# A transformer kernel on one core: thirty-two recorded orders instead of one, a rearranged head, column tiles from segment one, a last product cut 512 + 128

## The chip, the cores and the metric

One core of one Trainium2 chip runs the kernel. Its engines run on their own and wait for each other by semaphores: TensorE (PE for matmuls, PEld for weight loads), VectorE (DVE), ScalarE (ACT), GpSimd (POOL) and SyncE (SP, which here issues nearly all DMAs). The metric is device microseconds of one execution; before the change the median of three runs is 577.09 us (575.79 to 577.29).

## The reference

Two layers, each an attention with a compressive memory and a feed-forward part, on 2048 tokens of width 640, all in bf16. The tokens are cut in four segments of 512.

```python
def _A_ref(x, wq, wk, wv, wo, beta):          # 32 heads of 20, N = 4 segments of L = 512
    for s in range(N):
        logits = einsum('bhqd,bhkd->bhqk', qs, ks) * scale + mask      # causal, inside the segment
        a_dot = einsum('bhqk,bhkd->bhqd', softmax(logits), vs)
        pq = phi(qs)                                                   # t > 0 ? t + 1 : exp(t)
        a_mem = (pq @ M) / (pq . z + 1e-06)                            # memory of earlier segments
        outs.append(g * a_mem + (1.0 - g) * a_dot)                     # g = sigmoid(beta), per head
        pk = phi(ks); M = M + pk^T vs; z = z + sum(pk)
    return concat(outs) @ wo
def _B_ref(x, w1, w2):
    return relu(x @ w1) @ w2                                           # 640 -> 1728 -> 640

x = x + _A_ref(_layernorm(x), wq, wk, wv, wo, beta)
x = x + _B_ref(_layernorm(x), w1, w2)
# and both once more, with the same weights
```

## The kernel before

**Recorder.** The program is not written in the order in which it runs. Some thirty Python generators ("streams") each describe one kind of work for all eight (layer, segment) pairs: scores, exponentials, causal masks, values, output projection, normalization, projections, feed-forward and so on. A stream yields an `Op` (engine, planned duration, tokens that it waits for), a `Need` (an event that another stream sets) or an `Acq` (a buffer slot). `Sched.run` keeps a planned clock for each engine and, step by step, takes the op that could start earliest; among equal starts the lower number given in `S.add` goes first. It appends the op to that engine's list with its semaphore waits (`Prog`). The order on each engine, and on SP's DMA queue, is therefore fixed by planned times, and each engine then runs its list strictly in order.

Some rules bend that choice. An op of PE that is not a score is held back (`late`) until what it waits for has been done for a guard time, `TRUST_NS` (0.4 us for ACT, DVE and POOL, 1 us for a DMA). A matmul block in another tiling mode than the last costs `SWITCH_NS` more; blocks in column tiles are held up to 4 us to join a score block. Where the plan leaves PE idle for 0.3 us or more, `keep_busy` puts small matmuls on the identity there (L594).

**Work.** PSUM has eight banks: two pairs (X, Y) for scores and four (`MISC`) for all else; the memory read uses one of those alone. A segment's attention goes in four steps (`m`) of two half-groups of four heads (`z`), each step in five rounds of scores (L1067, four heads side by side in row tiles), exponentials on ACT (L1119) and causal selects on POOL (L1131). Then come the values. In segments 0 and 1 of the first layer (`BY_TOKEN`) this is `values_by_token`: 40 matmuls of 21 columns per half-group (L1161), which leave numbers and denominators by token, and DVE divides straight from PSUM (L1173, L1174, L1177). In all others `apply` computes the transposed result with 16 matmuls in four column tiles (L1210), evacuates it to `av` (L1218 DVE or L1219 ACT), a DMA transpose on SP turns it to `avt` (L638), and `divide` works from there (L1246, L1247, L1254). `combine` adds the memory part (L1272). After that come turn_o, the output projection, the second normalization and the feed-forward product.

The memory read is L960, L968, L970 and L971, its update L1011 to L1032. Queries and keys go through a scratch tensor in HBM (`spill`, L856; `fill`, L903) into padded tiles `pad`, four slots; only the first heads go straight there (L883). `group` (L607 first matmul, L610 the rest) is the helper for all other products, `add_half` (L1281) adds a product to the residual, and L1379 stores a finished token tile.

**Head.** `first_ln_a` normalizes token tiles 0 and 1: statistics of both (L618, L620), one `lnU` (L628), one power on POOL (L632), two normalizations (L672). `first_ln_b` does tiles 2 and 3 with their statistics on ACT (L722, L729, then L630). PE transposes all four (L695), ACT or DVE evacuates them (L702, L701), and the projections begin. `consts` makes the constants: identity (L540), the mask `maskg` (memset L547, ten selects L552 and L555), the ones in the value tiles (memsets L562 and L564), the gates (L569 to L581). `warm_pe` (L590) runs 60 matmuls to begin with.

Of the kernel before, what the change touches and what calls it, by code (L numbers as in the profile page):

```python
# [11 lines left out]
H = 32  # L12
# [146 lines left out]
SWITCH_NS = 97.0  # L159
JOIN_NS = 4000.0  # L160
# [8 lines left out]
class Sched:  # L169


    def __init__(self, prog):
        self.P = prog
        self.free = {e: 800.0 for e in ENGS}
        self.t = {}
        self.events = {}
        self.streams = []
        self.dma_free = 0.0
        self.pe_mode = "full"
        self.spare = []  # L180
        self.idle_fn = None

    def keep_busy(self, op, start):
# [10 lines left out]
        if n > 1:  # L194
            self.P.waits("pe", s.tks)
            for _ in range(n):
                self.P.op("pe", lambda e, ap=s.ap: self.idle_fn(e, ap), False)
# [45 lines left out]
    def _alts(self, op):  # L243
# [7 lines left out]
        for k, (e, hold, fns, tail) in enumerate(op.alts):  # L251
            m = PE_MARGIN if e == "pe" else 0.0
            if e == "pe" and op.mode != self.pe_mode:
                hold = hold + SWITCH_NS
            start = max([self.at(t) + SEM_NS + m for t in waits], default=0.0)
            start = max(self.free[e], start)
            res.append((start + hold, start, k, e))
        return res

    def run(self):  # L260
        while True:
# [21 lines left out]
            for prio, n, st, alts, op, late in heads:  # L283
# [4 lines left out]
                if prio > 0 and alts and alts[0][3] == "pe":  # L288
                    sure = max([self.at(t) + TRUST_NS[self.P.lane(t)] for t in op.waits], default=0.0)
# [28 lines left out]
            if e == "pe":  # L318
                self.keep_busy(op, start)
            self.P.waits(e, waits)  # L320
# [10 lines left out]
            else:  # L331
# [6 lines left out]
                out = marks[0] if len(marks) == 1 else (marks or None)  # L338
            st[2], st[3] = None, ((slot, out) if slot is not None else out,)

# [31 lines left out]

def bass_interleave_layers__memory_aug_infini_attn__dense_activation_relu__prompt_kernel(
    nc, A_x, A_wq, A_wk, A_wv, A_wo, A_beta, B_x, B_w1, B_w2, out,
):
    with contextlib.ExitStack() as es:
        sb = lambda name, shape, dtype=dt.bfloat16: es.enter_context(nc.sbuf_tensor(name, shape, dtype))
        sem_ = lambda name: es.enter_context(nc.semaphore(name))
        P = Prog({e: sem_("clk_" + e) for e in ["act", "dve", "pool", "pe"]})
        S = Sched(P)  # L380


        NPAD, NXT, NXN, NPT = 4, 2, 2, 2
        wq_r = sb("wq_r", [128, FC, D])
        wk_r = sb("wk_r", [128, FC, D])
        wv_r = sb("wv_r", [128, FC, D])
        wo_r = sb("wo_r", [128, FC, D])
        w1_r = sb("w1_r", [128, FC, DFF])
        w2_r = sb("w2_r", [128, NDC, D])
        w2_u = sb("w2_u", [128, D])  # L390
        ident = sb("ident", [128, 128])
        warm = sb("warm", [128, 1], dt.float32)
        asum = sb("asum", [128, 4], dt.float32)
        beta_bc = sb("beta_bc", [128, H])
        gt = sb("gt", [128, 3, H], dt.float32)
        omg = sb("omg", [128, G, NJ, 4, 1], dt.float32)
        maskg = sb("maskg", [128, MW])
        stats6 = sb("stats6", [128, TT, 2, 6], dt.float32)
        mv = sb("mv", [128, TT, 2], dt.float32)
        rstd = sb("rstd", [128, TT], dt.float32)  # L400
        lnU = sb("lnU", [128, TT], dt.float32)
        mhalf = sb("mhalf", [128, 4], dt.float32)
        x_sb = sb("x_sb", [128, TT, D])
        xnT = sb("xnT", [128, NXT, NJ * FC, 128])
        xn_tok = sb("xn_tok", [128, NXN, 2 * D])
        stg = sb("stg", [128, FC, 2, L])
        phs = sb("phs", [128, FC * L])
        pad = sb("pad", [128, NPAD, 2, 2, L])
        rtmp = sb("rtmp", [128, 3, L])
        phk = sb("phk", [128, FC, NJ, 128])  # L410
        v_aug = sb("v_aug", [128, 2, NJ, H, DH + 1])
        M_sb = sb("M_sb", [128, MW], dt.float32)
        BD = sb("BD", [128, MW])
        PT = sb("PT", [128, NPT, 4, PTH])
        o_sb = sb("o_sb", [128, NJ, D])
        om_sb = sb("om_sb", [128, NJ, D])
        rden = sb("rden", [128, 2, 2 * NJ, 4, 1], dt.float32)
        av = sb("av", [128, 2, L])
        avt = sb("avt", [128, 2 * NJ, 128])
        rmem = sb("rmem", [128, 4, 16, 1], dt.float32)  # L420
        oT = sb("oT", [128, NJ * FC, 128])
        hT = sb("hT", [128, NFULL, L])
        hL = sb("hL", [128, 2 * 128])
        ps = es.enter_context(nc.psum_tensor("ps", [128, 8, 512], dt.float32))

        X = Slot(ps[:, 0:2, :], "SX")
        Y = Slot(ps[:, 2:4, :], "SY")
        MISC = [Slot(ps[:, 4 + k, :], "misc%d" % k) for k in range(4)]
        XNT_A = [Slot(xnT[:, k], "xnT_a") for k in range(1)]
        XNT_B = [Slot(xnT[:, k], "xnT_b") for k in range(1, NXT)]  # L430
        XN = [Slot(xn_tok[:, k], "xn") for k in range(NXN)]
        xn_sem = {id(s): sem_("xn%d" % k) for k, s in enumerate(XN)}
        early_w = w2_r[:].rearrange("p c d -> p (c d)")
        VLEN = NJ * H * (DH + 1)
        STGS = [stg, early_w[:, VLEN:VLEN + 2 * FC * L].rearrange("p (c n t) -> p c n t", c=FC, n=2)]
        STG = [[[Slot(ap[:, c, n], "stg") for c in range(FC)] for n in range(2)] for ap in STGS]
        PAD = [Slot(pad[:, k], "pad") for k in range(NPAD)]
        pad_sem = {id(s): sem_("pad%d" % k) for k, s in enumerate(PAD)}
        scr = nc.dram_tensor("scr", [2, D, 2 * L], dt.bfloat16, kind="Internal").ap()
        scr_sem = [[sem_("scr%d_%d" % (n, c)) for c in range(FC)] for n in range(2)]  # L440
        RT = [Slot(rtmp[:, k], "rt") for k in range(3)]
        PARTS = ((0, 1, 2), (3, 4))
        PHK = [Slot(phk[:, cs[0]:cs[-1] + 1], "phk") for cs in PARTS]
        PHS = [Slot(phs[:, cs[0] * L:(cs[-1] + 1) * L], "phs") for cs in PARTS]
        VAUG = [v_aug[:, k] for k in range(2)]
        VAUG += [early_w[:, 0:VLEN].rearrange("p (j h e) -> p j h e", j=NJ, e=DH + 1)]
        VA = [Slot(ap, "va") for ap in VAUG]
        BDS = Slot(BD, "bd")
        PTS = [Slot(PT[:, k], "pt") for k in range(NPT)]
        OSB = Slot(o_sb[:], "osb")  # L450
        OMS = [Slot(om_sb[:, :, 320 * k:320 * k + 320], "om") for k in range(2)]
        RDEN = [Slot(rden[:, k], "rden") for k in range(2)]
        AV = Slot(av[:], "av")
        AVT = Slot(avt[:], "avt")
        avt_sem = sem_("avt")
        RMEM = [[Slot(rmem[:, 2 * n + k], "rmem") for k in range(2)] for n in range(2)]
        OT = [Slot(oT[:, 2 * FC * k:2 * FC * k + 2 * FC], "oT") for k in range(2)]
        ot_sem = {id(s): sem_("ot%d" % k) for k, s in enumerate(OT)}
        phk_sem = [sem_("phk%d" % p) for p in range(2)]
        HT = Slot(hT, "hT")  # L460
        XNT_E = [Slot(hT[:, FC * k:FC * k + FC, :].rearrange("p c (i n) -> p (c i) n", n=128), "xnT_e")
                 for k in range(2)]


        def ld(e, name, nbytes, fn, waits=()):
            tk = yield dma(e, sem_("d_" + name), nbytes, fn, waits, lat=2200.0)
            S.set(name, tks=[tk])

        def wload(e, name, w, src, waits=()):
            yield from ld(e, name, 819200, lambda eng: eng.dma_start(  # L470
                w[:], src.rearrange("(c p) d -> p c d", p=128)), waits)

        xs = A_x[0].rearrange("(t p) d -> p t d", p=128)

        def loads():
            def x_pair(name, t):
                yield from ld("sp", name, 327680, lambda e: e.dma_start(x_sb[:, t:t + 2, :], xs[:, t:t + 2, :]))

            def cols(name, w, src, c0, c1):
                yield from ld("sp", name, 1280 * (c1 - c0), lambda e: e.dma_start(  # L480
                    w[:, :, c0:c1], src.rearrange("(c p) d -> p c d", p=128)[:, :, c0:c1]))

            yield from x_pair("x00", 0)
            yield from x_pair("x01", 2)
            yield from cols("wk0", wk_r, A_wk, 0, 256)
            yield from cols("wq0", wq_r, A_wq, 0, 256)
            yield from cols("wk1", wk_r, A_wk, 256, D)
            yield from cols("wq1", wq_r, A_wq, 256, D)
            yield from wload("sp", "wv", wv_r, A_wv)
            yield from x_pair("x10", 4)  # L490
            yield from x_pair("x11", 6)

# [244 lines left out]
        def proj_ln(a, s):  # L737
            if (a, s) == (0, 0):
                return
# [720 lines left out]
```

## Time and profile before

| | |
|---|---|
| median of three runs | 577.09 us (575.79 to 577.29) |
| the profiled execution's own time | 575.81 us |
| its span, first to last instruction | 573.8 us |
| mean granted TensorE clock | 0.997 |
| PE busy | 564.1 us, 98% of the span |
| PEld, DVE, ACT, POOL busy | 313.4, 407.3, 409.0, 188.4 us |
| DMA | 59.90 MB, mean 104 GB/s |

A row of the timeline gives start, length, engine, source line, operation, output <- input and count; rows of one kind in a row are merged. A row of a table of stretches gives from:to, the length, the busy time of each engine with its count of instructions, the granted clock, the DMA share and GB/s. A row of the groups gives a line's operation, shapes and count, then busy us and the mean ns of one, then the idle time before it and what ended that. Matmuls are pipelined: the length of one includes its way through the array, so what a block costs PE is the distance from its start to the next start.

### The profile page before, as it was taken

What the parts mean: (1) busy time and instruction counts of PE and PEld (TensorE: products, weight loads), DVE (VectorE), ACT (ScalarE), POOL (GpSimd) and SP (SyncE); (2) the same over time, 40 slices, a digit from 0 to 9 for tenths busy, and PEclk for the clock granted to TensorE, in tenths of its full rate; (3) what the DMA queues carried; (4) which work ended last, traced back from release to release, by engine and by line L of the source; (5) the groups of instructions that cost most, each with busy time, mean ns of one, the idle gap of its engine ahead of it and who ended that gap; (6) DMA issues with size and microseconds to landing.
All of it is one profiled execution on the core that took longest, in us unless ns stands there. A gap on an engine that the chain in (4) does not pass through costs nothing.

```text
span 573.8 us, 13249 instructions
## 1 busy us (share of the span) xinstructions
PE 564.1 (98%) x5448; PEld 313.4 (55%) x5448; DVE 407.3 (71%) x1053; ACT 409.0 (71%) x520; POOL 188.4 (33%) x293
## 2 busy tenths in 40 slices
PE   8999989999999999999999999999999999999998
PEld 7764545546554454555446545466445553665655
DVE  4789899956889687788699896699735776552202
ACT  5699998787787878878898677787866787313140
POOL 5234343433434334444433352043420433200000
PEclk9999998999999999999999999999999999999999
DMA  8478987742081443825159031781307420422101
GB/s 263 115 193 177 232 213 149 149 124 70 23 199 42 89 66 97 190 46 111 38 167 174 20 65 38 175 148 33 70 19 170 137 55 18 88 70 47 47 0 47
DMA packets 125725, 59.90 MB, mean 104 GB/s; under 512 B 104546, under 2 KB 115554, under 8 KB 125666
## 3 DMA queue, kind: packets, MB, share of 16 engines
q1 hardware_dynamic: 125536, 58.90, 43.9%
q8 instruction: 43, 0.70, 0.5%
q10 hardware_dynamic: 130, 0.16, 0.2%
q14 instruction: 16, 0.13, 0.1%
HBM read 20.57 MB, written 12.85 MB: 58 GB/s over the span
## 4 chain that ended last, share of the span: by engine, by line
PE 83%; DVE 11%; DMA 3%; ACT 2%; issue 0%; SPq 0%; POOL 0%
PE ps L610 54%; PE ps L607 11%; PE ps L1067 8%; PE ps L1210 5%; PE ps L1161 2%; PE ps L960 2%; DVE stats L618 2%; DVE stg L783 1%; PE ps L1011 1%; ACT PT L1119 1%; PE ps L1329 1%; DMA avt<-av 1%; DMA scr<-w_r 1%; DVE xn_tok L660 1%; DVE rtmp L926 1%; DVE x_sb L1281 1%
## 5 line engine op out<-in xcount | busy, mean ns | idle before, releaser
L1119 ACT ACTIVATE PT<-ps 128x1024 bf16<-128x1024 f32 x320 | 310.2, 1022 | 71.1 <-PE ps L1067 69.5
L1131 POOL TENSOR_SCALAR_AFFINE_SELECT PT<-PT 128x512 bf16<-128x512 bf16 x256 | 165.0, 662 | 287.6 <-ACT PT L1119 287.5
L610 PE MATMUL ps<-w_r,hT 128*128 128x320 bf16 x768 | 123.3, 299 | 0.0
L610 PE MATMUL ps<-xnT,w_r 128*128 128x512 bf16 x416 | 114.1, 380 | 0.0
L1281 DVE TENSOR_TENSOR x_sb<-x_sb,ps 128x320 bf16<-128x320 bf16 x128 | 60.0, 478 | 69.2 <-PE ps L610 68.6
L610 PEld LDWEIGHTS ps<-w_r,hT 128*128 128x128 bf16 x768 | 73.3, 98 | 31.3 <-issue 4.5
L1360 ACT ACTIVATE hT<-ps 128x512 bf16<-128x512 f32 x55 | 32.7, 597 | 45.8 <-PE ps L610 45.5
L1067 PE MATMUL ps<-pad 20*128 20x384 bf16 (+3 forms) x1024 | 64.4, 302 | 0.4 <-ACT PT L1119 0.2
L610 PEld LDWEIGHTS ps<-xnT,w_r 128*128 128x128 bf16 x416 | 39.4, 98 | 43.1 <-issue 4.1
L618 DVE BATCH_NORM_STATS2 stats<-x_sb 128x6 f32<-128x320 bf16 x124 | 55.6, 471 | 4.3 <-DMA x_sb<-in_A_x_dram 3.9
L610 PE MATMUL ps<-wo_r,oT 128*128 128x320 bf16 x256 | 47.0, 303 | 0.0
L1067 PEld LDWEIGHTS ps<-pad 20*128 20x128 bf16 x1024 | 18.1, 92 | 51.3 <-ACT PT L1119 24.4
L1358 DVE TENSOR_SCALAR hT<-ps 128x512 bf16<-128x512 f32 x49 | 33.3, 680 | 12.5 <-PE ps L610 12.4
L1218 DVE CAST av<-ps 128x512 bf16<-128x512 f32 x45 | 30.7, 683 | 15.9 <-PE ps L1210 15.8
L607 PE MATMUL ps<-xnT,w_r 128*128 128x512 bf16 x104 | 39.6, 381 | 0.0
L610 PE MATMUL ps<-wv_r,xnT 128*128 128x320 bf16 x192 | 35.5, 300 | 0.0
L610 PE MATMUL ps<-xnT,wk_r 128*128 128x512 bf16 (+1 forms) x140 | 35.5, 349 | 0.0
L1210 PE MATMUL ps<-PT,v_aug 128*32 128x512 bf16 (+4 forms) x768 | 34.9, 302 | 0.0
L610 PE MATMUL ps<-xnT,wq_r 128*128 128x512 bf16 (+1 forms) x140 | 34.3, 349 | 0.0
L783 DVE CAST stg<-ps 128x512 bf16<-128x512 f32 (+1 forms) x44 | 27.2, 617 | 10.0 <-PE ps L610 9.8
L928 ACT ACTIVATE stg<-stg 128x512 bf16<-128x512 bf16 x50 | 30.6, 634 | 3.1 <-DVE rtmp L926 3.0
L610 PEld LDWEIGHTS ps<-wo_r,oT 128*128 128x128 bf16 x256 | 24.7, 99 | 12.3 <-issue 2.9
(117 smaller groups left out, 702.2 us busy)
## 6 DMA issues: line engine op xcount, KB each, us to landing
pad<-scr SPq DMA_DIRECT2D x124, 80.0 KB
scr<-stg SPq DMA_DIRECT2D x34, 256.0 KB, 3.1
out_dram<-x_sb SPq DMA_DIRECT2D x16, 160.0 KB, 1.8
w_r<-in_B_w_dram SPq DMA_DIRECT2D x10, 216.0 KB, 4.2
w_r<-in_B_w_dram SPq DMA_DIRECT2D x13, 160.0 KB, 2.8
x_sb<-in_A_x_dram SPq DMA_DIRECT2D x4, 320.0 KB, 6.1
x_sb<-in_A_x_dram SPq DMA_DIRECT2D x8, 160.0 KB, 3.7
scr<-w_r SPq DMA_DIRECT2D x5, 256.0 KB, 4.2
```

The costliest lines, as they stand in the source:

```text
L607: bk, tk = yield pe(mm_ns(n), [(lambda e, bk, a=a, b=b: e.matmul(bk.ap[:, 0:n] if len(b.shape) == 2 else bk.ap[:, 0:n].rearrange("p (i n) ...
L610: tk = yield pe(mm_ns(n), [(lambda e, k=k, a=a, b=b, bk=bk: e.matmul(bk.ap[:, 0:n] if len(b.shape) == 2 else bk.ap[:, 0:n].rearrange("p (i ...
L618: tk = yield dve(320, 1, lambda e, c2=c2: e.bn_stats(stats6[:, t, c2, :], x_sb[:, t, c2 * 320:(c2 + 1) * 320]), xt)
L783: te = yield evac(N, 1, lambda e, sg=sg, bk=bk: e.tensor_copy(sg.ap[:, t0:t0 + N], bk.ap[:, 0:N]), lambda e, sg=sg, bk=bk: e.activation(sg ...
L1067: fns.append([(lambda e, z=z, j=j, hh=hh, N=N, o=o, sl=sl: e.matmul(ps[:, hh, o:o + N], sl.ap[32 * hh:32 * hh + DH, z, 0, 128 * j:128 * j ...
L1119: tx = yield act(1024, lambda e, dst=dst, src=src: e.activation(dst, src, ACT.Exp, scale=SCALE), sc + pw)
L1131: tm = yield pool(600.0, lambda e, reg=reg: e.affine_select(out=reg, in_=reg, pattern=[[0, 4], [1, 128]], compare_op=ALU.is_ge, fill=0.0, ...
L1210: fns.append((lambda e, bk, j=j, hh=hh, pt=pt, g=g0 + z: e.matmul(bk.ap[32 * hh:32 * hh + wide(g, hh), 128 * j:L], VAUG[vx(a, s)][:, j].re ...
L1218: te = yield evac(L, 1, lambda e, sl=sl, z=z, bk=bk: e.tensor_copy(sl.ap[:, z], bk.ap), lambda e, sl=sl, z=z, bk=bk: e.activation(sl.ap[:, ...
L1281: ta = yield dve(320, 1, lambda e: e.tensor_tensor(x_sb[:, t, 320 * hf:320 * hf + 320], x_sb[:, t, 320 * hf:320 * hf + 320], bk.ap[:, 0:32 ...
L1358: th = yield evac(512, 1, lambda e, dc=dc, bk=bk: e.tensor_scalar(hT[:, dc, :], bk.ap[:, :], 0.0, None, ALU.max), lambda e, dc=dc, bk=bk: ...
L1360: lambda e, dc=dc, bk=bk: e.activation(hT[:, dc, :], bk.ap[:, :], ACT.Relu), [tk] + HT.tks)
```

## The change

The body of the kernel function becomes a function `plan`, unchanged but for what follows, which is called 32 times with the same tensors and semaphores (`once` makes each only the first time). Each call records a whole program with another price of a mode change in the recorder's choice (`STARTS`: 97 ns plus -12 to +11.25 ns). `late` replays the recorded list with each DMA landing 500 ns later than planned, and the program whose replay ends first is emitted. The guard time now covers the slot's last users (a PSUM bank's evacuation) beside the op's inputs. `proj_ln`, the normalization ahead of the projections, moves from number 5 to 3, before phi and the memory's work (4).

In the head, the two memsets of ones wait for the evacuations of all four first token tiles, and the mask's operations stand behind them in the stream; tiles 0 and 1 get a `lnU` and a power each. Segment 1 of the first layer leaves `BY_TOKEN`. The last token tile's product is cut 512 + 128 instead of 320 + 320, with a store for each part. Two planned durations change (power 1000 to 760 ns, the DVE form of an evacuation in the head).

```diff
+STARTS = [SWITCH_NS + 0.75 * (k - 32 // 2) for k in range(32)]
+LATE_NS = 500.0
...
             if e == "pe" and op.mode != self.pe_mode:
-                hold = hold + SWITCH_NS
+                hold = hold + self.switch
...
-                    sure = max([self.at(t) + TRUST_NS[self.P.lane(t)] for t in op.waits], default=0.0)
+                    sl = self._pick(op.acq).tks if op.acq is not None else []
+                    sure = max([self.at(t) + TRUST_NS[self.P.lane(t)] for t in op.waits + sl], default=0.0)
...
+    def late(self):
+        free = {e: 800.0 for e in ENGS}
+        t = {}
+        dma_free = 0.0
+        for e, hold, tail, waits, out, is_dma in self.log:
+            m = SEM_NS + (PE_MARGIN if e == "pe" else 0.0)
+            start = max([t[id(k[0]), k[1]] + m for k in waits], default=0.0)
+            start = max(free[e], start)
+            free[e] = start + hold
+            if is_dma:
+                dma_free = max(dma_free, start + 300.0) + tail[1]
+                land = max(dma_free, free[e]) + tail[0] + LATE_NS
+                if tail[2]:
+                    free[e] = max(free[e], dma_free)
+            else:
+                land = free[e] + tail
+            for k in out:
+                if k is not None:
+                    t[id(k[0]), k[1]] = land
+        return max(t.values())
...
             S.set("mhalf", tks=[th])
+            xt0 = yield Need("xt", 0, 0, 0)
+            xt1 = yield Need("xt", 0, 0, 1)
+            t2 = yield pool(1200, lambda e: e.memset(
+                v_aug[:].rearrange("p b j h e -> p (b j h) e")[:, :, DH:DH + 1], 1.0), xt0 + xt1)
+            t3 = yield pool(1000, lambda e: e.memset(
+                VAUG[2].rearrange("p j h e -> p (j h) e")[:, :, DH:DH + 1], 1.0))
+            for b in range(3):
+                VA[b].tks = [t3 if b == 2 else t2]
             t3 = yield pool(700, lambda e: e.memset(maskg[:], 1.0))
...
-            t2 = yield pool(400, lambda e: e.memset(
-                v_aug[:].rearrange("p b j h e -> p (b j h) e")[:, :, DH:DH + 1], 1.0))
-            t3 = yield pool(250, lambda e: e.memset(
-                VAUG[2].rearrange("p j h e -> p (j h) e")[:, :, DH:DH + 1], 1.0))
...
-            tk = yield pool(1000, lambda e: e.tensor_tensor(rstd[:, sl], lnU[:, sl], mhalf[:, 0:n], ALU.pow), [tk] + h)
+            tk = yield pool(760, lambda e: e.tensor_tensor(rstd[:, sl], lnU[:, sl], mhalf[:, 0:n], ALU.pow), [tk] + h)
...
-            aggr = []
+            tch = []
             for t in range(2):
                 tk = yield from stats(t, w)
-                aggr.append(tk)
-            tch = yield from chain(0, 2, aggr)
+                tk = yield from chain(t, 1, [tk])
+                tch.append(tk)
             yield from first_pair(0, tch)
...
-        BY_TOKEN = ((0, 0), (0, 1))
+        BY_TOKEN = ((0, 0),)
...
-                for hf in range(2):
-                    bk, tk = yield from group(MISC, 320, [
-                        hid(i, dc) + (w2_part(i, dc)[:, hf * 320:(hf + 1) * 320], [hr[dc]])
+                cuts = (0, 512, D) if final and t == TT - 1 else (0, 320, D)
+                for c0, c1 in zip(cuts, cuts[1:]):
+                    bk, tk = yield from group(MISC, c1 - c0, [
+                        hid(i, dc) + (w2_part(i, dc)[:, c0:c1], [hr[dc]])
                         for dc in range(NDC)], w2t)
-                    ta = yield from add_half(t, hf, bk, tk)
+                    ta = yield from add_half(t, c0, bk, tk, n=c1 - c0)
                     tks.append(ta)
+                    if final and (c1 == D or t == TT - 1):
+                        o0 = c0 if t == TT - 1 else 0
+                        S.last = yield dma("sp", dout, 256 * (c1 - o0), lambda e, t=t, o0=o0, c1=c1: e.dma_start(
+                            out[0, t * 128:(t + 1) * 128, o0:c1], x_sb[:, t, o0:c1]), tks)
...
-        S.add(5, each(proj_ln))
+        S.add(3, each(proj_ln))
...
+        plans = [plan(k, sb, sem_, psum, dram, A_x, A_wq, A_wk, A_wv, A_wo, A_beta, B_x, B_w1, B_w2, out) for k in STARTS]
+        S = min(plans, key=lambda p: p.late())
```

1893 lines of the change are left out of this document (951 added, 942 removed).

## The prediction

> **What bounds the kernel now.** I read the page first (engines, slices, chain), then a table of stretches, the timeline of the head, the groups by shape, and the waits of TensorE. The page:
>
> ```profile
> span 573.8 us, 13249 instructions
> PE 564.1 (98%) x5448; PEld 313.4 (55%) x5448; DVE 407.3 (71%) x1053; ACT 409.0 (71%) x520; POOL 188.4 (33%) x293
> PE 83%; DVE 11%; DMA 3%; ACT 2%; issue 0%; SPq 0%; POOL 0%
> ```
>
> TensorE is busy for 564.1 of 573.8 us and carries 83% of the chain, so over most of the span only less work on PE, or fewer holes in it, shortens anything. The table shows where the holes are. Columns: stretch, its length, busy time of PE, PEld, DVE, ACT, POOL, granted clock, DMA share, GB/s.
>
> ```profile
> 20.00:80.00 60.00, 59.78 (x701) 34.21 (x697) 51.27 (x141) 54.43 (x73) 22.11 (x34) 1.00 0.80 194
> 80.00:84.00 4.00, 3.38 (x81) 2.60 (x76) 3.97 (x14) 3.48 (x5) 2.60 (x4) 1.00 0.89 290
> 84.00:88.00 4.00, 2.89 (x64) 2.04 (x65) 3.49 (x11) 3.79 (x5) 1.95 (x4) 0.93 1.16 196
> 88.00:92.00 4.00, 4.00 (x29) 2.16 (x29) 2.99 (x11) 3.19 (x5) 1.76 (x3) 0.65 0.96 194
> 92.00:104.00 12.00, 11.81 (x166) 6.99 (x163) 12.00 (x40) 10.39 (x13) 4.68 (x7) 1.00 0.35 73
> 104.00:112.00 8.00, 6.99 (x107) 4.33 (x105) 7.76 (x20) 5.54 (x7) 3.77 (x6) 1.00 0.98 176
> 112.00:500.00 388.00, 386.44 (x3675) 202.24 (x3674) 292.96 (x736) 301.04 (x364) 142.08 (x216) 1.00 0.41 93
> 500.00:574.00 74.00, 71.10 (x456) 43.13 (x453) 20.61 (x50) 16.29 (x28) 1.01 (x1) 1.00 0.15 41
> ```
>
> Before 20, PE waits for the first normalized tokens (rows below). From 20 to 80 it is full. From 80 to 112 it runs dry: idle (4 - 3.38) + (4 - 2.89) + (12 - 11.81) + (8 - 6.99) = 2.9 us, and the clock loses 0.35 x 4 + 0.07 x 4 = 1.7 us. From 112 on PE is full again until the tail. DVE is the tight engine of the dry stretch: 3.97 + 3.49 + 2.99 + 12.00 + 7.76 = 30.2 of 32 us; ACT has 26.4.
>
> **The change part by part.** Planning estimates alone also change (the power's, the evacuation's); they do nothing but move work. Durations are of the profiled execution: 575.81 us, span 573.8, 1.28 us under the median of the runs, 577.09.
>
> *Head.* Timeline (start, length) of the work around the first pair:
>
> ```profile
> 6.96 1.24 POOL L562 MEMSET v_aug<- 128x256 bf16 x1
> 7.04 2.27 DVE L672 TENSOR_SCALAR xn_tok<-x_sb,mv,rstd 128x640 bf16<-128x640 bf16 x2
> 7.78 1.00 POOL L564 MEMSET w_r<- 128x128 bf16 x1
> 9.23 0.16 DVE L630 TENSOR_SCALAR lnU<-asum 128x2 f32<-128x2 f32 x1
> 10.26 0.80 DVE L672 TENSOR_SCALAR xn_tok<-x_sb,mv,rstd 128x640 bf16<-128x640 bf16 x2
> 11.69 1.31 ACT L702 ACTIVATE xnT<-ps 128x640 bf16<-128x640 bf16 x2
> 19.64 1.01 POOL L632 TENSOR_TENSOR rstd<-lnU,mhalf 128x4 f32<-128x4 f32 x1 [9.48 <-DVE lnU L628]
> 19.90 0.39 PE L1067 MATMUL ps<-pad 20*128 20x512 bf16 x4
> ```
>
> The two normalizations of the first pair take 2.27 us where those of the second take 0.80, and the two memsets run beside just the slow pair (6.96 to 8.78). With the memsets gone from there the pair is done up to 2.27 - 0.80 = 1.5 us sooner.
>
> One chain per token tile adds a lnU of about 0.2 us on DVE (0.16 at 9.23) and a power of at most 1.01 us on POOL, and lets tile 0 start before tile 1's statistics are through: from nothing to -0.5 us. But keys and queries of the first two column chunks, and so the first scores (19.90), need both pairs. The second pair's lnU starts at 9.23, when DVE comes free of the first (7.04 + 2.27), and so gains at most the same 1.5 and at least nothing. I take -1.2 us, nearer to the 1.5 since the slow pair stands in front of both; bounds 0 (loads or pads are late instead) and -2.0.
>
> SBUF — State Buffer (section "Who interferes with whom") of the Trainium skill calls it a lock: GpSimd and VectorE in a two-port mode hold one port pair in turn, and the second waits for the whole of the first. By that rule the full 1.5 us come back and the whole sum below would be -5.4; the rows agree so far as the second pair, with nothing of POOL's beside it, takes 0.80.
>
> The new place costs POOL 1.24 + 1.00 us, and the mask's memset and ten selects go behind them. All wait for the second pair's evacuation (13.00 now). Queued behind on POOL is the next segment's power at 19.64; 13.0 + 2.24 + 0.73 + 10 x 0.37 = 19.7, so it just fits, and a miss costs that power some tenths. Rows for these terms:
>
> ```profile
> L547 POOL MEMSET maskg<- 128x756 bf16 x1 | 0.7, 727 | 0.0
> L552 POOL TENSOR_SCALAR_AFFINE_SELECT maskg<-maskg 128x147 bf16<-128x147 bf16 x4 | 1.5, 372 | 0.1
> ```
>
> *Column tiles in segment one.* One half-group by token and one by columns, each with what follows on PE (timeline), and how many there are (the line's own view):
>
> ```profile
> 128.87 1.16 PE L1161 MATMUL ps<-v_aug,PT 128*128 128x21 bf16 x40
> 129.89 0.38 PE L607 MATMUL ps<-xnT,w_r 128*128 128x512 bf16 x1
> 144.84 0.73 PE L1210 MATMUL ps<-PT,v_aug 128*32 128x512 bf16 x16
> 145.50 0.31 PE L607 MATMUL ps<-wo_r,oT 128*128 128x320 bf16 x1
> L1161 PE MATMUL ps<-v_aug,PT x320: 171/172/186, 86.8 to 136.1; 128*128 128x21 bf16 x160
> ```
>
> From start to next start: 1.02 us by token, 0.66 by columns with the change of tiling in it. Segment one has 320/40 = 8 such blocks: 8 x 0.36 = -2.9 us of PE. Half of them, before 112, lie in the dry stretch, where PE work is not always the limit; the other half is worth its full -1.4. I take -2.0; bounds -1.4 and -2.9.
>
> What it adds elsewhere (groups; count, busy and mean ns):
>
> ```profile
> L1218 DVE CAST av<-ps 128x512 bf16<-128x512 f32 x45 | 30.7, 683 | 15.9 <-PE ps L1210 15.8
> L1173 DVE RECIPROCAL rden<-ps 128x16 f32<-128x16 f32 x16 | 4.0, 249 | 5.2 <-PE ps L1161 5.2
> L1174 DVE TENSOR_TENSOR rden<-rden,omg 128x16 f32<-128x16 f32 x16 | 4.1, 258 | 0.3
> L1177 DVE TENSOR_TENSOR o_sb<-ps,rden 128x320 bf16<-128x320 f32 x16 | 7.7, 483 | 0.3
> L1246 DVE RECIPROCAL rden<-avt 128x32 f32<-128x32 bf16 x24 | 8.2, 342 | 3.4 <-DMA avt<-av 3.3
> L1247 DVE TENSOR_TENSOR rden<-rden,omg 128x32 f32<-128x32 f32 x24 | 7.3, 303 | 0.3
> L1254 DVE TENSOR_TENSOR o_sb<-avt,rden 128x320 bf16<-128x320 bf16 x48 | 25.1, 550 | 0.3
> L638 SPq DMA_TRANSPOSE avt<-av x24: 1232/1233/1470, 154.8 to 497.1; - x24
> ```
>
> Per pair of half-groups DVE goes from 2 x (0.249 + 0.258 + 0.483) = 1.98 us to 2 x 0.683 + 0.342 + 0.303 + 2 x 0.550 = 3.11: +1.1 us, four times +4.5. Two pairs fall before 112, +2.3 where DVE has 1.8 us left; ACT, with 5.6 left, can take evacuations, so I put nothing down. SP issues four transposes more, 4 x 1.23 us, each behind an evacuation, with pad fills and weight loads queued behind them; four pads are filled ahead, which hides it.
>
> *The order.* Thirty-two plans, a changed cost of a mode change in the choice alone, a guard time on freed PSUM banks, and normalization raised over the memory's work change no operation, only its place. What they can win is what the dry stretch loses (filler matmuls by window, their timeline, PE's waits in 80 to 112):
>
> ```profile
> 80.00:112.00 32.00, 3.26 (x43) 2.49 (x43) 0.95 0.75 156
> 81.95 0.62 PE L594 MATMUL ps<-ident 128*128 128x128 bf16 x8
> PE ps L960 <- DVE om_sb L971: 1.5, 3, 0.9
> ```
>
> A filler steps at (0.62 - 0.22)/7 = 0.057 us, 0.22 being the first one's length; 43 are 2.4 us. Idle 2.9, clock 1.7 and fillers 2.4 make 7.0 us, the most that order can win here. The guard aims at the 1.5 us in which PE stood in the memory read for a bank that DVE had not freed, right ahead of the stretch at 0.65 of the clock. I take -1.6 us, the price of about one such slow stretch; bounds -7.0 and, below nothing, +6.8 (first rival).
>
> *Tail.*
>
> ```profile
> 571.13 0.49 DVE L1281 TENSOR_TENSOR x_sb<-x_sb,ps 128x320 bf16<-128x320 bf16 x1 [1.42 <-PE ps L610]
> 571.65 0.33 SPq L1379 DMA_DIRECT2D out_dram<-x_sb  x1
> ```
>
> PE streams 2 x 320 or 512 + 128 columns, the same total. The last addition, 0.49 us at 320 wide, takes between 0.20 (in proportion) and 0.49 at 128 wide; midway it is 0.3, an estimate: -0.2. The store after it takes 573.8 - 571.65 = 2.15 us and moves a fifth of the bytes: 0 to -0.4. I take -0.3 in all, near the addition's part, since how much of 2.15 us goes with the bytes no row shows; the cover for the 512-wide part is the 128-wide product behind it, and without it this is +0.2. DMA: Bandwidth & Descriptors (section Specifications) of the Trainium skill wants 512 bytes or more per transfer and names a read-modify-write below that; the last store writes 256 bytes a row, so by that rule its gain could be lost and the tail would be -0.2.
>
> Sum: -1.2 - 2.0 - 1.6 - 0.3 = -5.1 us. 575.81 becomes 570.7, the median 577.09 becomes **572.0 us**; its own range is 569 to 575.
>
> **The rivals.** Under 0.3%, 1.7 us here, nothing can be told from no change.
>
> *Slower: normalization crowds DVE.* A segment's normalization costs DVE
>
> ```profile
> L618 DVE BATCH_NORM_STATS2 stats<-x_sb 128x6 f32<-128x320 bf16 x124 | 55.6, 471 | 4.3 <-DMA x_sb<-in_A_x_dram 3.9
> ```
>
> 8 x 0.47 us of statistics and, with two normalizations per pair at 0.80, aggregation and lnU, some 6.4 to 6.8 us. Put ahead of the memory read where DVE has 1.8 us left, it delays the read, segment one's result and PE's next work by as much. Fully exposed: +6.8 - 1.2 - 1.4 - 0.3 = +3.9, so 581 us. It decides from 2.9 us exposed on. For it: DVE at 12.00 of 12 us. Against it: that normalization already runs there, and done earlier it would lie in 20 to 80, with 8.7 us free. Chance 0.16.
>
> *Nothing much: the gains are swallowed.* If the dry stretch only moves (PE gets there sooner and waits longer), head, early columns and order are worth nothing and -1.4 - 0.3 is left: 575.4. Against it: ACT and DVE, which bound that stretch, start sooner as well. Chance 0.16.
>
> *Large: the dry stretch closes.* -1.2 - 2.9 - 7.0 - 0.3 = -11.4: 565.7. Against it: 43 fillers say that the recorder itself saw no work to put there. Chance 0.13.
>
> **How the numbers follow.** The forecast has 0.55. Faster: 0.55, 0.13 and a little of the second rival, 0.71; same 0.14, the rest of the second rival; slower 0.15, nearly all of the first, whose milder form ends near no change. The range goes from the large case to between the second and the first rival: 565.5 to 578.5.
>
> **What would show it.** Right: both first normalizations near 0.4 us and first scores near 18.7; 320 fewer matmuls of 21 columns, 8 column blocks more at 0.66 us; PE idle plus clock loss in 80 to 112 clearly under 4.6 us; a last addition under 0.3 us. Wrong: scores still near 19.9; a second stretch at half clock; PE waiting for evacuations or pads between 84 and 140; new holes after 112, where I assume none.

## The result and the profile after

The changed kernel takes 574.15 us in the median (572.77 to 575.32); run beside it, the kernel before takes 576.51 (575.64 to 577.29). The ratio is 0.9958, 95% interval 0.9942 to 0.9974: 0.42% faster, about 2.4 us. A repetition on another occasion gave 0.9957 (0.9939 to 0.9975). The prediction was 0.9% faster; sign right, size about half.

The page of the changed kernel; its profiled execution took 572.77 us:

```profile
span 571.0 us, 12994 instructions
PE 564.0 (99%) x5314; PEld 311.1 (54%) x5315; DVE 409.0 (72%) x1049; ACT 410.5 (72%) x525; POOL 191.6 (34%) x294
PE 80%; DVE 12%; DMA 5%; SPq 1%; POOL 1%; issue 0%; ACT 0%
```

TensorE is still the bound and its busy time has hardly moved (564.1 to 564.0 us), although 192 matmuls of work went (320 of 21 columns out, 128 in column tiles in). The table of stretches says what else has changed (columns as in the prediction: stretch, length, busy time of PE, PEld, DVE, ACT, POOL, granted clock, DMA share, GB/s):

```profile
20.00:80.00 60.00, 59.14 (x763) 35.57 (x761) 48.59 (x136) 52.41 (x71) 24.97 (x39) 1.00 0.83 194
80.00:84.00 4.00, 4.00 (x26) 1.79 (x25) 3.93 (x11) 3.13 (x4) 1.52 (x4) 1.00 0.91 178
84.00:88.00 4.00, 4.00 (x45) 2.04 (x45) 4.00 (x11) 4.00 (x7) 1.73 (x3) 1.00 1.12 192
88.00:92.00 4.00, 4.00 (x38) 2.37 (x32) 3.96 (x12) 3.88 (x6) 1.42 (x2) 1.00 1.05 271
92.00:104.00 12.00, 11.42 (x136) 6.25 (x135) 11.90 (x35) 10.96 (x15) 6.41 (x9) 1.00 0.82 156
104.00:112.00 8.00, 7.95 (x85) 3.73 (x83) 7.68 (x23) 7.28 (x10) 3.09 (x5) 1.00 0.36 82
112.00:500.00 388.00, 386.37 (x3601) 202.06 (x3600) 300.08 (x749) 301.97 (x368) 143.38 (x213) 1.00 0.43 96
```

From 80 to 112 PE is idle for 0.6 us (2.9 before), and the clock is full throughout (1.7 us lost before). That reads as a closed dry stretch. It isn't: the filler matmuls count as busy. Their own table by stretch (the fillers' line alone: PE and PEld busy, clock, DMA share, GB/s):

```profile
48.00:80.00 32.00, 3.32 (x47) 2.63 (x47) 1.00 0.93 209
80.00:112.00 32.00, 3.46 (x53) 3.13 (x53) 1.00 0.78 159
```

Before there were none from 48 to 80 and 43 from 80 to 112; now there are 47 and 53. The first of them starts at 55.17 us where it was 81.95: the dry stretch begins some 27 us earlier and is longer and shallower.

So that this can be summed, I took the trace of each kernel from one matmul's start to the next and sorted every piece. *Holes* are idle time of PE between its first and last matmul, fillers behind the 60 warming ones, and half of the time that PE works at half clock (counted as half the work). *Work* is all else up to the last matmul. In us of the profiled execution:

| | before | after | difference |
|---|---|---|---|
| holes, 0 to 20 us | 3.07 | 2.09 | -0.98 |
| holes, 20 to 112: idle + fillers + clock | 3.15 + 3.10 + 1.71 = 7.96 | 1.49 + 6.44 + 0 = 7.93 | -0.03 |
| holes, from 112 on | 1.83 | 2.62 | +0.8 |
| work: value blocks (by token and by columns) | 47.9 | 45.1 | -2.8 |
| work: all else | 508.8 | 509.4 | +0.6 |
| after the last matmul | 2.74 | 2.31 | -0.43 |
| span | 573.8 | 571.0 | -2.8 |

The last line holds 1.6 us ahead of the first matmul, the same in both.

The head, by the timeline (start, length; releaser in brackets):

```profile
6.52 0.44 DVE L700 TENSOR_SCALAR xn_tok<-x_sb,mv,rstd 128x640 bf16<-128x640 bf16 x1
7.42 0.45 DVE L700 TENSOR_SCALAR xn_tok<-x_sb,mv,rstd 128x640 bf16<-128x640 bf16 x1 [0.45 <-POOL rstd L660]
12.37 1.23 POOL L575 MEMSET v_aug<- 128x256 bf16 x1 [2.72 <-ACT xnT L730]
13.18 0.99 POOL L577 MEMSET w_r<- 128x128 bf16 x1
18.94 0.40 PE L1095 MATMUL ps<-pad 20*128 20x512 bf16 x4
```

The two normalizations of the first pair take 0.44 and 0.45 us, where they took 2.27 together; the memsets stand at 12.37 and 13.18; the first scores start at 18.94 instead of 19.90. A column block of segment one, and the tail (timelines; the store's row is the line's own view: count, then shortest, median and longest ns, first to last start):

```profile
127.91 0.73 PE L1238 MATMUL ps<-PT,v_aug 128*32 128x512 bf16 x16
128.57 0.39 PE L638 MATMUL ps<-xnT,w_r 128*128 128x512 bf16 x1
```

```profile
568.77 0.29 DVE L1309 TENSOR_TENSOR x_sb<-x_sb,ps 128x128 bf16<-128x128 bf16 x1
L1408 SPq DMA_DIRECT2D out_dram<-x_sb x3: 332/332/426, 565.5 to 569.1; - x3
```

### The profile page after: what moved, and what is told of

The parts are those of the page before. It is cut to its first block, busy times and chain, and to the rows that moved or that the text cites. A ratio compares the mean times of both kernels' runs of the same rounds, so it can differ in the third digit from the quotient of the medians.

```text
span 571.0 us, 12994 instructions
## 1 busy us (share of the span) xinstructions
PE 564.0 (99%) x5314; PEld 311.1 (54%) x5315; DVE 409.0 (72%) x1049; ACT 410.5 (72%) x525; POOL 191.6 (34%) x294
## 4 chain that ended last, share of the span: by engine, by line
PE 80%; DVE 12%; DMA 5%; SPq 1%; POOL 1%; issue 0%; ACT 0%
PE ps L638 52%; PE ps L635 10%; PE ps L1095 7%; PE ps L1238 6%; DVE stats L646 2%; DVE xn_tok L688 2%; DMA hT<-xn_tok 2%; DMA xnT<-xn_tok 2%; DMA x_sb<-in_A_x_dram 1%; PE ps L988 1%; PE ps L1039 1%; PE ps L1189 1%; DVE stg L811 1%; DVE x_sb L1309 1%; PE ps L1357 1%; DVE hT L1386 1%
## 5 line engine op out<-in xcount | busy, mean ns | idle before, releaser
L1159 POOL TENSOR_SCALAR_AFFINE_SELECT PT<-PT 128x512 bf16<-128x512 bf16 x256 | 167.3, 672 | 282.9 <-ACT PT L1147 282.5
L638 PE MATMUL ps<-w_r,hT 128*128 128x320 bf16 (+2 forms) x768 | 123.4, 299 | 0.1
L1309 DVE TENSOR_TENSOR x_sb<-x_sb,ps 128x320 bf16<-128x320 bf16 (+1 forms) x128 | 60.2, 480 | 64.9 <-PE ps L638 64.1
L1388 ACT ACTIVATE hT<-ps 128x512 bf16<-128x512 f32 x58 | 34.8, 599 | 50.0 <-PE ps L638 49.8
L1095 PE MATMUL ps<-pad 20*128 20x512 bf16 (+3 forms) x1024 | 64.8, 301 | 0.1
L1246 DVE CAST av<-ps 128x512 bf16<-128x512 f32 x51 | 34.8, 682 | 21.5 <-PE ps L1238 21.4
L1238 PE MATMUL ps<-PT,v_aug 128*32 128x256 bf16 (+5 forms) x896 | 40.7, 302 | 0.3
L1386 DVE TENSOR_SCALAR hT<-ps 128x512 bf16<-128x512 f32 x46 | 31.4, 683 | 8.2 <-PE ps L638 7.9
L688 DVE TENSOR_SCALAR xn_tok<-x_sb,mv,rstd 128x640 bf16<-128x640 bf16 x60 | 29.9, 529 | 2.3 <-POOL rstd L660 2.1
L811 DVE CAST stg<-ps 128x512 bf16<-128x512 f32 (+1 forms) x40 | 25.3, 634 | 8.4 <-PE ps L638 8.2
```

The source lines that it names most:

```text
L638: tk = yield pe(mm_ns(n), [(lambda e, k=k, a=a, b=b, bk=bk: e.matmul(bk.ap[:, 0:n] if len(b.shape) == 2 else bk.ap[:, 0:n].rearrange("p (i ...
L688: nm = lambda e, bx, t, k: e.tensor_scalar(bx.ap[:, k * D:k * D + D], x_sb[:, t + k, :], mv[:, t + k, 0:1], rstd[:, t + k:t + k + 1], ALU. ...
L1095: fns.append([(lambda e, z=z, j=j, hh=hh, N=N, o=o, sl=sl: e.matmul(ps[:, hh, o:o + N], sl.ap[32 * hh:32 * hh + DH, z, 0, 128 * j:128 * j ...
L1159: tm = yield pool(600.0, lambda e, reg=reg: e.affine_select(out=reg, in_=reg, pattern=[[0, 4], [1, 128]], compare_op=ALU.is_ge, fill=0.0, ...
L1238: fns.append((lambda e, bk, j=j, hh=hh, pt=pt, g=g0 + z: e.matmul(bk.ap[32 * hh:32 * hh + wide(g, hh), 128 * j:L], VAUG[vx(a, s)][:, j].re ...
L1246: te = yield evac(L, 1, lambda e, sl=sl, z=z, bk=bk: e.tensor_copy(sl.ap[:, z], bk.ap), lambda e, sl=sl, z=z, bk=bk: e.activation(sl.ap[:, ...
```

## The experiments

Each ratio is to the kernel before, run in between on the same chip.

**1. Other plans of the changed rules.** The recorder chose the eleventh of 32 (92.5 ns). Three others emitted instead:

```diff
-STARTS = [SWITCH_NS + 0.75 * (k - 32 // 2) for k in range(32)]
+STARTS = [SWITCH_NS + 0.75 * (k - 32 // 2) for k in [30]]      # [16], [3]
```

> The changed kernel, but only the plan with the price 107.5 ns for a mode change is recorded, which the kernel's own replay ranks last of the 32 (9.1 us behind the one it emits). Theory A, the choice among plans is worth what the replay says: some 9 us slower than the changed kernel, near 583. Theory B, PE has a fixed amount of work and the plans differ only by noise: within 2 us of the changed kernel, 572 to 576.

> The changed kernel, but only the plan with the unchanged price of 97 ns is recorded; all other edits stay. The replay puts it 3.0 us behind the emitted plan. Theory A: about 577, so that the choice among 32 is the whole gain over the kernel before. Theory B: within 1 us of the changed kernel; the gain comes from the head, the columns and the tail.

> The changed kernel with only the plan of 87.25 ns, second best by the replay, 1.0 us behind the emitted one. If the replay ranks plans: within 2 us of the changed kernel's ratio of 0.9958. If plans are a draw: somewhere between 0.995 and 1.006, the spread of the two plans already run.

Plan 30: 576.86 us, ratio 0.9997 (0.9978 to 1.0016). Plan 16: 579.61, 1.0057 (1.0032 to 1.0083). Plan 3: 576.57, 0.9987 (0.9970 to 1.0004). The same operations under the same rules thus spread over 1%, more than twice the gain. Plan 30 and plan 16 come out as neither of their two theories said; plan 3 lies within both of its own. By the accounting above their holes are 18.1, 21.9 and 16.7 us, against 12.6 in the plan that was chosen. The waits of PE in plan 16 (waiting tile and line, releaser, us in total, times, longest) show the memory read and a late transfer in them:

```profile
PE ps L988 <- DVE om_sb L999: 3.3, 5, 1.2
PE ps L1095 <- DMA pad<-scr: 2.1, 2, 1.5
```

The kernel's own replay put plans 10, 3, 16 and 30 at 571.5, 572.4, 574.5 and 580.5 us. It named the best of the four, but had plan 30 6 us behind plan 16, while on the chip 30 is the faster.

**2. The choice alone.** The old rules and operations, with the 32 plans and the choice by replay added (it takes the nineteenth):

```diff
+STARTS = [SWITCH_NS + 0.75 * (k - 32 // 2) for k in range(32)]
...
+        S = min(plans, key=lambda p: p.late())
```

> The kernel before, old rules and old head, with nothing added but the 32 plans and the choice by the replay. The replay's best is 0.7 us ahead of the plan that the kernel before uses. If choosing among plans is worth something by itself: 1 to 3 us faster than before. If it is only one more draw: anywhere from 3 us faster to 3 us slower, and the replay says nothing about which.

577.45 us, ratio 1.0013 (0.9998 to 1.0027): by itself the search brought nothing here, in the one plan that it chose. Eleven of this kernel's twelve executions had a mean clock of 1.000, the kernel before beside it in four of 35; so a clock that stays up is not a gain by itself. By the accounting above, its profiled execution has 14.1 us of holes and 1.1 us more work than the kernel before.

**3. Segment one by token again.**

```diff
-    BY_TOKEN = ((0, 0),)
+    BY_TOKEN = ((0, 0), (0, 1))
```

> The changed kernel with segment one by token again (32 plans, one chosen). PE has 8 x 0.36 = 2.9 us more to do. If that work lies on the path: 2 to 3 us slower than the changed kernel, near 577. If the column tiles' saving was swallowed by the dry stretch (filler matmuls took its place): within 1 us, and clearly fewer fillers than 145.

573.02 us, ratio 0.9935 (0.9911 to 0.9958): at least as fast as with the column tiles. PE does 2.3 us more work, and its holes are 11.0 us instead of 12.6, with 127 fillers instead of 145. What the column tiles take from PE's work is not needed for the gain.

**4. The memsets alone.** The kernel before, with its order on every queue held; only the memsets wait as in the changed kernel, and the fillers of the head are left out.

```diff
+            xt0 = yield Need("xt", 0, 0, 0)
+            xt1 = yield Need("xt", 0, 0, 1)
...
-                v_aug[:].rearrange("p b j h e -> p (b j h) e")[:, :, DH:DH + 1], 1.0))
+                v_aug[:].rearrange("p b j h e -> p (b j h) e")[:, :, DH:DH + 1], 1.0), xt0 + xt1)
...
-        if gap < IDLE_NS or self.idle_fn is None:
+        if gap < IDLE_NS or self.idle_fn is None or start < 20000.0:
```

> The kernel before with its whole order held instruction by instruction; only the two memsets of ones are moved on POOL behind the evacuations of the four first token tiles, and the 40 fillers of the head are left out (they would hold PE until 8.6 us). If the memsets blocked DVE: the first pair's two normalizations take 0.8 us instead of 2.27, the first transposes start near 7.5 instead of 9.01, first scores 0.5 to 1.5 us before 19.9. If that gain goes through to the end: 1 us faster than before, near 576; if it is swallowed between 50 and 112 us: the same time within 0.4 us.

576.28 us, ratio 1.0006 (0.9987 to 1.0025). The timeline of this kernel:

```profile
7.32 0.80 DVE L694 TENSOR_SCALAR xn_tok<-x_sb,mv,rstd 128x640 bf16<-128x640 bf16 x2 [0.52 <-POOL rstd L654]
9.26 0.27 PE L629 MATMUL ps<-xnT,wk_r 128*128 128x256 bf16 x1 [0.63 <-ACT xnT L724]
19.63 0.40 PE L1089 MATMUL ps<-pad 20*128 20x512 bf16 x4
```

In the kernel before, the first projection is this row:

```profile
10.66 0.27 PE L607 MATMUL ps<-xnT,wk_r 128*128 128x256 bf16 x1
```

The memsets were what made the first pair slow (2.27 to 0.80 us), and the first projection starts 1.4 us sooner (9.26; 10.66 before). But with the old order behind it, the first scores gain only 0.27 us, where 0.5 to 1.5 were expected, and the end nothing that can be told; the interval would still allow 0.7 us.

**5. No fillers behind the head.** The changed kernel's own order, without the fillers that its plan put in after 20 us.

```diff
-        if gap < IDLE_NS or self.idle_fn is None:
+        if gap < IDLE_NS or self.idle_fn is None or start > 20000.0:
```

> The changed kernel's own order, with the filler matmuls behind the head (planned start after 20 us) left out: 109 fewer, about 6.1 us of PE steps. If they only stand in holes that PE has anyway: the same time within 1 us, PE idle up by about 6 us, and slower by 1.7 us for each stretch in which the clock now falls. If they push real work back: up to 6 us faster, near 568.

577.18 us, ratio 1.0001 (0.9978 to 1.0024): the whole gain is gone. The mean granted clock of its twelve executions is 0.988 to 0.997; all eight of the changed kernel have 1.000. Its stretches (columns as above):

```profile
64.00:68.00 4.00, 2.86 (x57) 1.56 (x57) 0.77 (x4) 4.00 (x6) 1.85 (x3) 0.90 0.95 192
68.00:72.00 4.00, 4.00 (x27) 1.91 (x21) 3.56 (x8) 2.68 (x4) 1.50 (x2) 0.67 0.91 262
100.00:104.00 4.00, 2.80 (x37) 0.95 (x31) 3.96 (x13) 3.69 (x5) 2.96 (x4) 1.00 0.30 68
104.00:108.00 4.00, 2.31 (x11) 0.99 (x12) 3.86 (x12) 3.81 (x5) 1.56 (x3) 0.60 0.97 193
108.00:112.00 4.00, 4.00 (x34) 1.47 (x33) 2.86 (x8) 2.67 (x4) 0.80 (x2) 0.55 0.26 57
```

Where the fillers were, PE is idle, and behind the holes the clock falls to half, for 3.4 us at 67.2 and for 6.8 us at 104.8. By the accounting, 7.4 us of fillers become 8.1 us of idle time, and the half clock adds 4.7 us of the 6.7 by which this profiled span (577.8 us) is longer than the changed kernel's. So the fillers stood in holes that PE has anyway, and most of what they are worth here is the clock. What PE waits for from 20 to 112, exponentials above all:

```profile
PE ps L1095 <- ACT PT L1147: 4.4, 5, 1.9
PE ps L635 <- DMA hT<-xn_tok: 1.5, 2, 0.9
PE ps L988 <- DVE om_sb L999: 0.8, 1, 0.8
```

**6. Is ScalarE what holds the dry stretch?** The kernel of 5, with the exponentials of scores steps 1 to 7 over half their width only; half of those probabilities are left out, and so the time stands for a faster ACT alone.

```diff
+                    if 0 < m < 8:
+                        w = 128 if u == 2 else 256
+                        dst, src = (dst[:, :, :, 0:w], src[:, :, :, 0:w]) if u == 2 else (dst[:, :, 0:w], src[:, :, 0:w])
```

> The run without fillers once more, in the same order, with the exponentials of steps 1 to 7 of layer one over half of their columns (0.6 us instead of 1.02; the other half of those probabilities is left out, so the output is not the reference's). If ACT is what PE waits for between 50 and 112 us: PE's waits for PT, 6.0 us, go, the clock stays up, and it is 4 to 8 us faster than the run without fillers, 569 to 573. If DVE or the DMAs hold the stretch: within 2 us of 577.

576.11 us, ratio 0.9992 (0.9974 to 1.0009). ACT is busy for 38.3 us of 50 to 112 instead of 54.5, and PE has 15.3 us of holes all the same (18.0 in 5). Two stretches, and what is left of PE's wait for the exponentials from 20 to 112:

```profile
96.00:100.00 4.00, 3.04 (x40) 0.96 (x37) 3.97 (x14) 2.40 (x5) 2.68 (x4) 1.00 0.50 101
100.00:104.00 4.00, 2.00 (x14) 0.85 (x11) 3.86 (x14) 3.56 (x7) 2.29 (x4) 0.58 0.82 156
PE ps L1095 <- ACT PT L1150: 2.8, 3, 1.3
```

The wait for the exponentials fell from 4.4 to 2.8 us, not to nothing, so ACT was eased and not taken out. DVE, at 3.97 and 3.86 of 4 us, remains full where PE is dry. ACT alone isn't what holds it; that DVE is was not tried by itself.

**7. Fillers into the holes of the kernel before.** Order held; 43 fillers at the seven holes that its trace shows between 80 and 111 us.

```diff
+FILL = {894: 4, 941: 5, 960: 3, 976: 15, 1118: 3, 1228: 9, 1296: 4}   # position on PE: fillers
...
-        if gap < IDLE_NS or self.idle_fn is None:
+        extra = FILL.pop(self.P.pos["pe"] - self.put, 0)
+        if self.idle_fn is None or (gap < IDLE_NS and not extra):
             return
...
+        n += extra
```

> Order and queues exactly those of the kernel before; 43 filler matmuls are put into seven holes of TensorE that its trace shows between 80 and 111 us (the longest, 0.9 us ahead of a memory read at 85, gets 15). Nothing else changes. Theory: half of the gain of the changed kernel is the clock. Its 145 fillers keep TensorE full from 52 to 112 us, so the 3.4 us at half clock that most executions of the kernel before show near 87 us don't come. Then 43 fillers alone take the mean clock of most runs from 0.997 to 1.000 and the time falls by about 1.2 us, to a ratio of 0.998 (0.9965 to 0.9990). Rival: the fall of the clock doesn't hang on these holes; the mean clock stays at 0.997 or below, and the ratio is 1.000 (0.9990 to 1.0015, the upper end if a filler holds up the read behind it).

577.05 us, ratio 1.0009 (0.9992 to 1.0025). The theory failed in its result. Of twelve executions five had the full clock, of 35 of the kernel before eight. The profile of one execution shows what went wrong there. First its stretches:

```profile
84.00:88.00 4.00, 3.95 (x76) 3.08 (x76) 3.49 (x12) 3.79 (x5) 2.11 (x4) 1.00 1.14 191
88.00:92.00 4.00, 4.00 (x49) 2.42 (x46) 3.97 (x14) 3.89 (x7) 2.00 (x3) 1.00 0.95 206
104.00:108.00 4.00, 2.58 (x36) 1.41 (x34) 3.96 (x9) 2.82 (x3) 1.59 (x3) 1.00 0.80 174
108.00:112.00 4.00, 4.00 (x65) 3.50 (x62) 2.82 (x8) 1.94 (x2) 1.07 (x2) 0.65 0.82 187
```

And what PE waits for from 104 to 112:

```profile
PE ps L620 <- DVE stg L809: 1.4, 1, 1.4
```

At 84 to 92 it works: PE full, clock 1.00 where it was 0.93 and 0.65. But at 106 a filler itself (L620) waits 1.4 us for its PSUM bank, which DVE frees late; that opens a larger hole than the one it was to fill, and the half clock comes there. So it doesn't tell whether well-placed fillers would give the 1.2 us. (The expectation's 145 fillers of the changed kernel count 36 of the head; 100 lie between 48 and 112. And that the half clock comes near 87 us in most executions of the kernel before is not shown: the one trace shows it there, of the others only the mean clock is known.)

**8. A wider search, by a harder replay.** Experiment 3's rules; of 96 switch values the one at 78.25 ns, good in both replays.

```diff
-STARTS = [SWITCH_NS + 0.75 * (k - 32 // 2) for k in range(32)]
+STARTS = [78.25]
...
-    BY_TOKEN = ((0, 0),)
+    BY_TOKEN = ((0, 0), (0, 1))
```

> The changed rules with column tiles from segment two on, as in the kernel before, and one plan out of 96 switch values (78.25 ns), picked by a replay that is harder than the kernel's own (1.5 us late on each transfer, 90 ns on each semaphore, ScalarE 3% slower); the kernel's own replay puts it at 571.6 us. Theory: column tiles in segment one bring nothing, since the stretch is held by other engines, and what decides is the plan; a plan that stands up to the harder replay is no slower than the changed kernel: a ratio to before of 0.9935 (0.990 to 0.996). Rival: neither replay ranks plans on the chip, and this plan lies anywhere in the spread that four plans of the changed rules showed, 0.9958 to 1.0057, with its middle at 1.000.

579.05 us, ratio 1.0042 (1.0029 to 1.0056). The rival's forecast holds: a plan that was good in both replays is slower than the kernel before. Its waits of PE over the whole span:

```profile
PE ps L622 <- DVE stg L811: 1.9, 1, 1.9
PE ps L635 <- DMA hT<-xn_tok: 1.7, 2, 1.0
```

And two of its stretches:

```profile
104.00:108.00 4.00, 2.12 (x54) 1.53 (x54) 3.93 (x11) 2.38 (x4) 2.04 (x3) 1.00 0.82 158
108.00:112.00 4.00, 3.76 (x40) 3.07 (x39) 2.85 (x10) 2.17 (x3) 1.48 (x2) 0.57 0.83 92
```

Again a filler (L622) stands in front of a bank that isn't free, and half clock follows. With the same rules, experiment 3's plan gave 0.9935: 1.1% between two plans of one set of rules.

**9. The normalization's number put back.**

```diff
-    S.add(3, each(proj_ln))
+    S.add(5, each(proj_ln))
```

> The changed kernel with one number put back: the projections and normalizations stand at priority 5 again instead of 3; 32 plans, of which its own replay takes one at 573.3 us (1.9 us over that of the changed kernel). Theory: this number decides where TensorE runs dry. With 5 the fillers and holes lie again between 80 and 112 us, as in the kernel before, and none at 52 to 64, where the changed kernel has 47 fillers; fillers and holes together stay at some 12 us, so the time is within the spread of the plans: ratio 0.998 (0.994 to 1.004). Rival: earlier normalizations were a loss by themselves (they crowd VectorE); then it is faster than the changed kernel run beside it by over 0.2%, with holes and fillers together under 10 us.

576.97 us, ratio 0.9997 (0.9981 to 1.0014). The time lies in the theory's range, but its mechanism fell. The fillers by stretch:

```profile
48.00:80.00 32.00, 5.18 (x71) 3.99 (x71) 1.00 0.83 209
80.00:112.00 32.00, 2.73 (x40) 2.35 (x40) 1.00 0.80 159
```

71 fillers still lie between 48 and 80, so this number doesn't decide where PE runs dry; holes are 15.6 us, not 12. In experiment 8 and in plans 16 and 30 of experiment 1, all with the number at 3, there are none from 48 to 80. It hangs on the plan as a whole. Nor did the rival come true: without the earlier normalization the kernel is slower than the changed one, 576.97 us beside 573.75, though each side is one plan. Eleven of its twelve executions had the full clock, so here too that was not enough.

**10. The changed kernel again**, beside 7 to 9:

> The changed kernel itself, beside the other three on the same chip, so that they can be compared with it and not only with the kernel before. Both theories: a ratio of 0.9958 (0.994 to 0.9975) and a mean clock of 1.000.

573.75 us, ratio 0.9957 (0.9939 to 0.9975). All twelve executions had the full clock.

## Why the prediction was right, and by how much

The sum forecast was -5.1 us; the profiled execution went from 575.81 to 572.77, -3.0, and the medians by 2.4 and 3.0. By its terms:

*Head, -1.2.* Measured -0.98 us of holes up to 20 us. The mechanism was right, and so was the size at its place: 0.44 + 0.45 stand where 2.27 stood, and the pair is done at 7.87 instead of 9.31. SBUF — State Buffer (section "Who interferes with whom") of the Trainium skill calls it an exclusive lock; the traces agree, here and in experiment 4, as far as 2.27 us beside the memsets and 0.80 to 0.89 without them go. The -1.5 at the end that the prediction worked out beside it didn't come: 0.96 us of it was left at the scores, and 0.27 under the old order. What the head gives to the end by itself is below what experiment 4 can resolve.

*Columns, -2.0.* PE's value blocks fell by 2.8 us, close to the forecast's upper bound of 2.9; a block is 128.57 - 127.91 = 0.66 us, as said. That it ends up in the time isn't shown: by token, under another plan, the kernel was no slower (experiment 3), and two plans by token stand 1.1% apart. The term is real as work and undetermined as time.

*Order, -1.6.* **This is the term that was mis-sized.** In the prediction's words, it could win "what the dry stretch loses". The dry stretch lost 7.96 us before and loses 7.93 now. (The prediction put it at 7.0. It took the 43 fillers at 0.057 us each, 2.4 us; from start to start, with the last filler of a group at up to its whole 0.22 us, they are 3.1. The accounting also holds the 0.2 us of idle time from 20 to 80.) Idle time (-1.7) and half clock (-1.7) turned into fillers (+3.3). Behind it come 0.8 us of new holes, where the prediction assumed none, and 0.6 us more of all other work. Beside the other measured terms that leaves +1.4 where -1.6 stood. The step that failed was taking a hole's disappearance for a gain: fewer holes are worth something only if work moves into them, and here fillers did.

*Tail, -0.3.* Measured -0.43: the last addition went from 0.49 to 0.29 us, and the store from its issue to the end from 2.15 to 571.04 - 569.08 = 1.96. By DMA: Bandwidth & Descriptors (section Specifications) of the Trainium skill the store's gain could have been lost at 256 bytes a row; the trace shows no such loss, though the gain is only 0.2 us.

*The rivals.* "Normalization crowds DVE" didn't come about: DVE is fuller in 80 to 112 (3.93 + 4.00 + 3.96 + 11.90 + 7.68 = 31.5 of 32 us, 30.2 before), yet in 20 to 112 PE waits less for it at the memory read, 0.3 us where it was 1.5 (its waits in that stretch):

```profile
PE ps L988 <- DVE om_sb L999: 0.3, 1, 0.3
```

"The dry stretch only moves" was right in its mechanism: the stretch moved and its sum stayed. In its price it left out the head, but the measured -2.4 us lies nearer to its -1.7 than to the -5.1 that was forecast. "Large" was far off.

**What carries the 0.42%.** Two things are measured. The first is the clock. In the last comparison the kernel before had the full clock in 8 of 35 executions, with a median of 575.25 us, against 576.72 over all; the changed kernel had it in all 12, at 573.75. So at equal clock 1.5 of those 3.0 us are left, and about half of the gain goes with the half clock that no longer comes. That compares executions; the experiment to it is 5, where the half clock comes back without the fillers and the whole gain is gone. The 1.5 us at equal clock are the sum of less work, head and tail against new holes. The clock alone doesn't carry the gain either: plan 3 had it full in all twelve executions, experiments 2 and 9 in eleven of twelve, and none of them is faster than before by more than the measurement is uncertain. The second is the plan: of four measured plans of the changed rules one is faster than before by more than the measurement is uncertain, two are not told from it, and one is slower. That the replay emitted the fast one is in part luck: of these four it named the best, but it put experiment 8's plan at 571.6 us, next to this one's 571.5, and that took 579.05. Which of head, columns and guard the remaining 1.5 us belong to stays open. The guard was not tried alone: each change gives another plan, and plans of the same rules differ by more. No version beat the changed kernel beyond doubt. Experiment 3 stands at 0.9935 beside its 0.9958, with intervals that overlap.

## What to carry to other kernels

Where a recorder lays out the whole order, every change of a rule also draws a new plan; here plans of the same rules lay 1% apart, so measure several plans of each variant before an effect is put down to the rule, and choose the plan on the chip rather than by replay. Count fillers as holes when reading a busy PE, and place them only where their PSUM bank is certainly free. Cutting the last addition and moving POOL's work out of DVE's way gave at their own place what their rows said; how much of that reached the end was too small to be told.

## What was unexpected of the hardware

Half clock came in pieces of 3.4 us (6.8 in one place each of experiments 5 and 6), and the time from a trace's first clock event to each fall is a multiple of 3.41 us: 81.9 us in the kernel before, 102.4 in experiments 7 and 8. In the fourteen traces at hand, leaving out what comes after the last matmul, it fell eight times, always after a piece in which PE was busy for 52 to 67%, never after a fuller one; nine pieces in that range were not followed by a fall, so the share alone doesn't decide, and what does stays open. TensorE: Matmul & The Clock Gate (Part 1) of the Trainium skill gives the same free-running window, 3413 ns, and half rate after at least one idle window. The window agrees; the idleness doesn't, since PE was busy for over half of the window ahead of each fall. In time a fall is 1.7 us, 0.3% of this kernel. The kernel before has at least one in most executions, and in the last comparison its times go up as the clock goes down: 575.25 us at a mean clock of 1.000, 576.69 at 0.997, 577.13 at 0.994.
